# Strassen's scheme for one more unit's q, k, v projection, GpSimd allowed for the weights' low halves, and new priorities and waits in a planned kernel

## The chip, the cores and the metric

The kernel runs on one core of one Trainium2 chip. The metric is device time in microseconds (us), lower is better. The kernel before took 1135.82 us (median of 3 runs, 1135.46 to 1136.92).

## The reference

Two pairs of layers act on x of 2048 rows (tokens) by 640 columns. Each pair is an attention layer and an MLP layer, both with a layer norm in front and a residual sum behind. The attention is local and dilated: a token at position s looks at the 8 positions s, s-2, ..., s-14, in 32 heads of 20 columns. Both pairs use the same weights.

```
for layer in (A, B, A, B):          # A: attention, B: MLP
    A: q, k, v = layernorm(x) @ wqkv            # 640 -> 3 * 640
       logits  = sum(q[s] * k[s - 2 j]) / sqrt(20),  j = 0..7, masked where s - 2 j < 0
       x = x + (softmax(logits) . v[s - 2 j]) @ wo
    B: h = gelu(layernorm(x) @ w1 + b1)         # 640 -> 1536
       x = x + h @ w2 + b2                      # 1536 -> 640
```

All is float32. The kernel keeps the accuracy with pairs of float16: every matmul operand is split into a high half (the value rounded to float16) and a low half (what is left), and a product is three float16 matmuls: high by high, high by low, low by high.

## The kernel before, in words

**Units.** The 2048 rows are cut into 4 units of 512 rows (even or odd positions, first or second half), and the two pairs of layers make 8 units of work, numbered 0 to 7: units 0 to 3 are the first pair of layers, 4 to 7 the second, and unit 4 works on the rows of unit 0 when the MLP of unit 0 is done. A unit has 4 tiles of 128 rows, and its heads are taken in 4 groups of 8 heads (160 columns each of q, k and v). There are thus 32 attention groups.

**The steps of a unit.** The layer norm (`layernorm`) runs mostly on ScalarE (ACT): sums with `accum_out`, then the normalized rows, then their high half; the low half is a subtraction on VectorE (DVE, L648) or on GpSimd (POOL). DMA transposes bring the halves to `yT`. TensorE (PE) multiplies with the weights `wq` (L904, `qkv`), ACT evicts the result to `ev` (L924), a DMA writes it to a DRAM buffer `spill`, and two DMAs fetch it back with the neighbours that the window needs. The attention of a group is a chain on DVE (`attention`): the products of q and k (L998), their sum over each head (L1003), the softmax's small steps (L1010 to L1017, with the exponential on ACT), the products with v (L1019), three sums over the window (L1024 twice, L1027), and the low half of the output (L1035, on DVE or POOL). `project` transposes the output by DMA and multiplies it with `wo` on PE (L1056); its banks are first filled with x by ACT (L1068). Then comes the layer norm for the MLP and the MLP itself (`mlp`): 12 steps per unit of an inner product of 15 matmuls (L1123), a gelu and a rounding on ACT (L1129, L1132), a low half on DVE or POOL (L1134), and an outer product of 24 matmuls (L1144) into five accumulation banks `acc0` to `acc4`, the rest of the columns of all four tiles lying in `acc4`. Units 6 and 7 do their MLP together at the end, by Strassen's scheme (`pair`, `joint`).

**How the banks of the MLP go from unit to unit.** There is one set of the five banks. For units 0, 1 and 2 DVE adds each bank to x (L1188: `acc4` first, then `acc0` to `acc3`), and the next unit's outer product may start on a bank when DVE has read it. For the units from 3 on ACT writes x into the banks ahead (L1104 for `acc0` to `acc3`, L1106 for `acc4`), the outer product adds to that, and ACT takes the sum out. So the first matmul of unit 3's outer product waits for two drains on DVE (`acc4` and `acc0` of unit 2) and the two fills on ACT behind them.

**Strassen for q, k, v.** For the units of the list SEVEN (before: 5, 6 and 7) `qkv7` takes seven products P1 to P7 in place of eight, over two tiles of rows and two groups of columns at a time (L832): 54 matmuls of 480 columns for such a block, four blocks in a unit. A plain unit takes 15 matmuls for each of 16 pairs of tile and group. The scheme needs sums of rows, made on DVE (L679 to L686) and split once more (L706 on ACT, L708 on DVE or POOL), sums of the outputs on DVE (L864, four in a unit), and sums of weights. `factors` makes these after the last plain unit has used the weights: it writes the weights to DRAM (L749), loads pieces of the raw weights (L758), combines them on DVE (L766) and splits them on ACT and DVE (L778, L780).

**The weights of the MLP and of wo** are split once, early on (`prep_rows`, 29 tiles of 128 by 640): ACT writes the high half, 64 times the weight rounded (L500), and DVE writes 64 times the weight minus the high half in one instruction (L501). The MLP's weights then go to DRAM and come back from there.

**What sets the order.** The program is written down as a list of operations with an engine, an estimated duration, a priority, what they need and what buffers they use. `Plan.run` makes a list schedule of it with its own clock: each engine takes the operation that can start first, and between equals the one with the lower priority number. The instructions are then emitted in the order of the planned starts, and on the chip each engine goes through its own list in that order, waiting wherever the next one isn't ready. An operation made with `either` may go to DVE or to POOL; POOL takes it only while DVE is in a sum over heads (L1003), and HOLD says how long DVE leaves it alone first. AHEAD says how far the inner products of the MLP may run ahead of the outer ones.

Of the kernel before, what the change touches and what calls it, by code (L numbers as in the profile page):

```python
# [11 lines left out]
AF = mybir.ActivationFunctionType  # L12
# [11 lines left out]
WS = 64.0  # L24
# [14 lines left out]

AHEAD = 1.5  # L40

# [6 lines left out]

SEVEN = (5, 6, 7)
KH = 2  # L50
# [18 lines left out]

HOLD = {'s': 0.0, 'hlo': 2.0, 'a': 12.0, 'b': 0.0, 'xb': 50.0, 'ol': 12.0, 'ol3': 0.0}  # L70

# [6 lines left out]
class Plan:  # L78
# [49 lines left out]
    def run(self):  # L128
# [172 lines left out]
        order.sort(key=lambda o: o["at"])  # L301
        self.time = max(clock.values())
        self.order = order
        return order
# [15 lines left out]
def sliding_dilated_then_mlp_kernel(  # L320
# [115 lines left out]
    def act(n, prio, emit, need=(), give=(), use=(), table=None, ptr=0, acc=0):  # L436
        plan.add("act", a_cost(n, ptr, acc), prio, emit, need, give, use, table)
# [61 lines left out]
    def split(hi, lo, src):  # L499
        return (lambda: nc.scalar.activation(hi(), src(), AF.Copy, scale=WS),  # L500
                lambda: nc.vector.scalar_tensor_tensor(lo(), src(), WS, hi(), op0=OP.mult, op1=OP.subtract))  # L501
# [18 lines left out]
    def prep_rows(name, key, prio, src, hi, lo, use=(), first=0):  # L520
        def load():
            st = tile_of(*key)
            st = st.rearrange("p a c -> p (a c)").bitcast(FT) if len(st.shape) == 3 else st
            w = src()
            nc.sync.dma_start(st.rearrange("p (k c) -> p k c", k=w.shape[1]) if len(w.shape) == 3 else st, w)

        def raw():
            st = tile_of(*key)
            return st.rearrange("p a c -> p (a c)").bitcast(FT) if len(st.shape) == 3 else st

        dma(P * D * 4 / 1e3, prio, load, need=[("ev", 0, M - 1, 0)], give=[("st", name)], use=[key],
            packet=4 * P if name[0] == "m" and not name[2] else 4 * D)
        a, v = split(hi, lo, raw)
        act(D, prio + first, a, need=[("st", name)], give=[("hi", name)], use=[key, *use])
        dve(D, LOP, v, need=[("hi", name)], give=[("lo", name)], use=[key, *use])

# [33 lines left out]
    def layernorm(n, prio, yk, twice):  # L570
# [11 lines left out]
        def first(t):  # L582
            return prio if n or twice else (-1100, -995, -899, -898)[t]
# [45 lines left out]
        for t in range(m):  # L629
# [13 lines left out]
            if n == 0 and not twice:  # L643
# [3 lines left out]
                need=[("y", name, t)], give=[("yh", name, t)], use=[key, nk, hk])  # L647
            either(D, HOLD['b' if twice else 'a'], first(t), lambda eng, key=key, parts=parts: eng.tensor_sub(parts()[:, 1], tile_of(*key), parts()[:, 0]),  # L648
                need=[("yh", name, t)], give=[("yl", name, t)], use=[key, nk, hk])
# [92 lines left out]
    def factors():  # L742
# [3 lines left out]
        for p in range(2):  # L746
            for q, (g, k) in ORIGIN.items():
                size = 1 if q[0] == "R" else 2
                dma(P * size * 2 * C * 2 / 1e3, -22, lambda p=p, q=q, g=g, k=k, size=size: nc.sync.dma_start(  # L749
                    ws[p, q], flat(wq[:, 2 * p + g, k:k + size])), need=[("wq", 2 * p + g, i) for i in range(3)] + [("out", 0, NF - 1, 0) if p else ("qkvp", SEVEN[0] - 1, M - 1, 1)],  # L750
                    give=[("ws", p, q)], packet=size * 4 * C)
        gone = [("ws", 1, q) for q in ORIGIN]
        for p in (1, 0):
            for j in range(2):
# [12 lines left out]

                dve(4 * C, -24, combine, need=[("fr", p, j, i) for i in range(4)], give=[("fs", p, j)], use=[ak], more=0.2)
                for i, n in enumerate((3, 1)):
                    def part(a, i=i, j=j, p=p):  # L770
                        if p:
                            return wq[:, 2, 3, a] if i else wq[:, 2, :3, a]
                        return wq[:, 2, 2 + j, a] if i else wq[:, 1:4, j, a]

                    def whole(i=i, raw=raw):
                        return raw[3] if i else wq_blocks[:, A0:A0 + 6 * C].bitcast(FT).rearrange("p (i c) -> p i c", c=C)

                    act(n * C, -24, lambda part=part, whole=whole: nc.scalar.activation(part(0), whole(), AF.Copy, scale=WS),  # L778
                        need=[("fs", p, j), *plain(p)], give=[("fh", p, j, i)], use=[ak, tk])
                    dve(n * C, -24, lambda part=part, whole=whole: nc.vector.scalar_tensor_tensor(  # L780
                        part(1), whole(), WS, part(0), op0=OP.mult, op1=OP.subtract),
                        need=[("fh", p, j, i)], give=[("fl", p, j, i)], use=[ak, tk])
# [18 lines left out]
    def qkv7(n):  # L801
# [5 lines left out]
        for s, (p, b) in enumerate(order):  # L807
# [4 lines left out]
            e0, e1 = ("ev", (n, g0, b)), ("ev", (n, g1, b))  # L812
            prio = -500 + n + 0.01 * s

# [68 lines left out]
    def qkv(n):  # L883
# [10 lines left out]
        for k, (g, b) in enumerate(halves):  # L894
            ek = ("ev", (n, g, b))
            for i in range(2):
# [9 lines left out]

                prio, done = (-500 if n != NU - 1 else 13) + n + 0.01 * k, ("qkvp", n, t, g)
                if n or g:
# [642 lines left out]
    for n in range(N):  # L1551
        if n:
            layernorm(n, -100 + n, ("yT", ("a", n)), False)
        qkv(n)
        for g in range(NG):
            fetch(n * NG + g)
            attention(n * NG + g)
        project(n)
        layernorm(n, -150 + n, ("yT", ("b", n)), True)

# [43 lines left out]
```

## Time and profile before

| | |
|---|---|
| runs | 1135.46, 1135.82, 1136.92 us; median 1135.82 |
| the profiled execution | 1137.4 us; its span, from the first to the last instruction, 1135.6 us |
| PE busy | 1121.8 us, 99% of the span |
| DVE busy | 1043.6 us, 92% |
| ACT busy | 648.4 us, 57% |
| POOL busy | 149.9 us, 13% |
| granted PE clock | 1.000 on average |

The span is one execution under the profiler; the 1.8 us between its span and its time lie around the first and the last instruction. Matmuls overlap in the pipeline, so a matmul's own duration is longer than what it adds to a row of them; a chain row with a count gives what a group costs in sequence.

### The profile page before, as it was taken

What the parts mean: (1) busy time and instruction counts of PE and PEld (TensorE: products, weight loads), DVE (VectorE), ACT (ScalarE), POOL (GpSimd) and SP (SyncE); (2) the same over time, 40 slices, a digit from 0 to 9 for tenths busy, and PEclk for the clock granted to TensorE, in tenths of its full rate; (3) what the DMA queues carried; (4) which work ended last, traced back from release to release, by engine and by line L of the source; (5) the groups of instructions that cost most, each with busy time, mean ns of one, the idle gap of its engine ahead of it and who ended that gap; (6) DMA issues with size and microseconds to landing.
All of it is one profiled execution on the core that took longest, in us unless ns stands there. A gap on an engine that the chain in (4) does not pass through costs nothing.

```text
span 1135.6 us, 16918 instructions
## 1 busy us (share of the span) xinstructions
PE 1121.8 (99%) x6560; PEld 603.4 (53%) x6560; DVE 1043.6 (92%) x878; ACT 648.4 (57%) x1187; POOL 149.9 (13%) x109
## 2 busy tenths in 40 slices
PE   8999999999999999999999999999999999999998
PEld 6444455456554565455445544456446555645476
DVE  7999999999999999999999999999989995768972
ACT  6357356647572283757576773478636733857720
POOL 1105001302221011102011311121001210100000
PEclk9999999999999999999999999999999999999999
DMA  9999786678877859769787798567797756695101
GB/s 308 301 331 247 218 213 162 209 261 231 257 263 204 224 176 316 251 200 256 200 297 217 192 258 291 192 197 183 193 334 210 218 172 162 156 268 161 43 25 70
DMA packets 257564, 246.05 MB, mean 217 GB/s; under 512 B 150524, under 2 KB 215116, under 8 KB 257484
## 3 DMA queue, kind: packets, MB, share of 16 engines
q1 hardware_dynamic: 257484, 244.98, 73.6%
q8 instruction: 51, 0.84, 0.3%
q14 instruction: 29, 0.24, 0.1%
HBM read 157.55 MB, written 52.64 MB: 185 GB/s over the span
## 4 chain that ended last, share of the span: by engine, by line
PE 67%; DVE 21%; issue 5%; DMA 4%; ACT 2%; SPq 0%; POOLq 0%; POOL 0%; DVEq 0%; ACTq 0%
PE ps L904 20%; PE ps L1123 14%; PE acc L1144 12%; PE ps L1056 8%; PE ps L832 6%; DVE sm L1003 4%; DVE pr L1019 4%; PE acc L1325 3%; DVE pr L998 3%; PE ps L1360 2%; PE ps L1325 2%; DVE pr L1024 2%; DVE pr L1257 1%; DVE w L708 1%; DMA yT<-w 1%
## 5 line engine op out<-in xcount | busy, mean ns | idle before, releaser
L1144 PE MATMUL acc<-c,act 128*128 128x512 f16 (+1 forms) x1728 | 248.9, 299 | 0.2
L904 PE MATMUL ps<-wq,yT 128*128 128x480 f16 (+1 forms) x1230 | 245.6, 361 | 1.5 <-ACT wq L500 1.1
L1123 PE MATMUL ps<-yT,c 128*128 128x512 f16 x1080 | 243.7, 379 | 0.0
L1144 PEld LDWEIGHTS <-act 128*128 128x128 f16 x1728 | 135.9, 98 | 110.0 <-issue 0.4
L904 PEld LDWEIGHTS <-yT 128*128 128x128 f16 x1230 | 118.7, 98 | 124.9 <-issue 1.3
L1019 DVE TENSOR_TENSOR pr<-sm,v 128x5120 f32<-128x5120 f32 x32 | 175.5, 5485 | 0.4
L998 DVE TENSOR_TENSOR pr<-qk 128x5120 f32<-128x5120 f32 x32 | 175.5, 5483 | 0.4
L1003 DVE TENSOR_REDUCE sm<-pr 128x256 f32<-128x5120 f32 x32 | 175.2, 5476 | 0.1
L1123 PEld LDWEIGHTS <-c 128*128 128x128 f16 x1080 | 103.7, 98 | 121.5 <-DVE c L501 0.3
L1024 DVE TENSOR_TENSOR pr<-pr 128x2560 f32<-128x2560 f32 x64 | 137.6, 2150 | 0.2
L1056 PE MATMUL ps<-wo,yT 128*128 128x320 f16 x960 | 131.9, 299 | 1.9 <-ACT ps L1068 1.9
L1056 PEld LDWEIGHTS <-yT 128*128 128x128 f16 x960 | 93.8, 98 | 39.6 <-issue 1.6
L924 ACT ACTIVATE ev<-ps 128x480 f32<-128x480 f32 x80 | 45.4, 569 | 109.1 <-PE ps L904 108.6
L1129 ACT ACTIVATE act<-ps,b 128x512 f32<-128x512 f32 x72 | 49.3, 685 | 99.9 <-PE ps L1123 98.7
L615 POOL TENSOR_TENSOR ln<-ln,half 128x2 f32<-128x2 f32 (+1 forms) x31 | 57.9, 1869 | 346.1 <-ACT ln L612 346.1
L832 PE MATMUL ps<-wq,yT 128*128 128x480 f16 x396 | 85.1, 366 | 2.0 <-ACT ps L850 1.8
L841 ACT ACTIVATE ev<-ps 128x480 f32<-128x480 f32 x72 | 39.9, 567 | 52.2 <-PE ps L832 50.1
L832 PEld LDWEIGHTS <-yT 128*128 128x128 f16 x396 | 38.2, 98 | 43.0 <-issue 2.7
L832 PE MATMUL ps<-wq 128*128 128x480 f16 x252 | 54.5, 366 | 0.8 <-ACT ev L841 0.8
L1035 POOL TENSOR_TENSOR ohl<-w,ohl 128x640 f16<-128x640 f32 x17 | 23.8, 1403 | 204.5 <-DVE sm L1015 45.3
L602 ACT ACTIVATE junk<-xf,ln 128x640 f16<-128x640 f32 x57 | 46.8, 820 | 0.5
L1132 ACT ACTIVATE act<-act 128x512 f16<-128x512 f32 x72 | 45.1, 626 | 1.4
(221 smaller groups left out, 1269.4 us busy)
## 6 DMA issues: line engine op xcount, KB each, us to landing
c<-mw SPq DMA_DIRECT2D x126, 320.0 KB, 3.6
spill<-ev SPq DMA_DIRECT2D x64, 480.0 KB, 3.9
qk<-spill SPq DMA_DIRECT2D x32, 880.0 KB, 6.1
v<-spill SPq DMA_DIRECT2D x32, 880.0 KB, 5.2
qk<-spill SPq DMA_DIRECT2D x32, 320.0 KB, 3.5
c<-in_B_w_dram SPq DMA_DIRECT2D x24, 320.0 KB, 5.1
mw<-c SPq DMA_DIRECT2D x24, 320.0 KB, 4.8
pr<-in_B_w_dram SPq DMA_DIRECT2D x24, 320.0 KB, 3.9
```

The source lines that it names most:

```text
L615: pool(0.5, prio, lambda t0=t0, t1=t1: nc.gpsimd.tensor_tensor(col(2)[:, t0:t1], col(2)[:, t0:t1], half[:, t0:t1], op=OP.pow), need=[("vr" ...
L832: nc.tensor.matmul(ps, r(x_, j), w[:, j, y_], start=start and i == 0, stop=i == len(todo) - 1, skip_group_check=True)
L904: nc.tensor.matmul(ps, transposed(yk)[:, a * KD + k, t * P:(t + 1) * P], wq[:, g, k, b, i0 * GC:i1 * GC], start=first and j == 0, stop=las ...
L998: nc.vector.tensor_mul(pr.rearrange("p w t c -> p w (t c)"), w[:, HALO + m:HALO + 2 * m].rearrange("p t c -> p (t c)")[:, None, :].to_broa ...
L1003: dve(E, G - 0.7, lambda: nc.vector.tensor_reduce(by_key(), heads(), axis=AX.X, op=OP.add), need=[("qk", G)], give=[("lg", G)], use=[*pk, sk])
L1019: dve(E, G - 0.85, lambda: nc.vector.tensor_mul(heads(), by_key()[:, :, :, None].to_broadcast([P, W, m * GH, DH]), windows(tile_of(*vw), [ ...
L1024: dve(m * w * GC, G - 0.9, lambda w=w: nc.vector.tensor_add(pr[:, 0:w], pr[:, 0:w], pr[:, w:2 * w]), need=[last], give=[("ad", G, w)], use=vk)
L1056: nc.tensor.matmul(tile_of(*pk)[:, :D // 2], transposed(yk)[:, a * KD + k, t * P:(t + 1) * P], wo[:, b, k, c * D // 2:(c + 1) * D // 2], s ...
L1123: nc.tensor.matmul(tile_of(*pk)[:, :nt], tile_of(*ck)[:, a, k * P:(k + 1) * P], transposed(yk)[:, c * KD + k, t0 * P:t1 * P], start=i == 0 ...
L1129: act(nt, -430, lambda pk=pk, h32=h32, e=e: nc.scalar.activation(tile_of(*h32)[:, :nt], tile_of(*pk)[:, :nt], AF.Gelu_apprx_tanh, bias=b1[ ...
L1144: nc.tensor.matmul(accs[k][:, c0:c0 + n], tile_of(*hk)[:, a, (i - t0) * P:(i - t0 + 1) * P], tile_of(*wk)[:, c, w0:w0 + n], start=first, s ...
L1325: nc.tensor.matmul(tile_of(*to(i))[:, :HALF], hl()[:, a, i * P:(i + 1) * P], row(c), start=start and (a, c) == PASS[0], stop=(a, c) == PAS ...
```

## The change

It does five things.

- Unit 4 joins SEVEN, so its q, k, v go through `qkv7`, its rows through `sums_of_rows`, and the sums of weights in `factors` are due between unit 3's and unit 4's projections, where they were due between unit 4's and unit 5's.
- In `prep_rows` ACT first scales the raw weights in place (a new instruction), then rounds them; the low half becomes a plain subtraction made with `either`, so that POOL may take it. In the new file these are lines 542, 543 and 544.
- The priorities of the projections and of the layer norms are tables by unit (QKV_AT, ROWS_AT, INNER_AT) in place of formulas; PREP_AT takes the place of a number with the same value.
- HOLD gets new values, with one by unit for the low halves of the layer norm (HOLD_A); AHEAD goes from 1.5 to 2.5.
- The store of the second half of the plain weights waits for the first outer product of the MLP's first step, where it waited for the last step of unit 0.

```diff
-AHEAD = 1.5
+AHEAD = 2.5
-SEVEN = (5, 6, 7)
+SEVEN = (4, 5, 6, 7)
-HOLD = {'s': 0.0, 'hlo': 2.0, 'a': 12.0, 'b': 0.0, 'xb': 50.0, 'ol': 12.0, 'ol3': 0.0}
+HOLD = {'lo': 0, 's': 2, 'hlo': 0, 'b': 0, 'xb': 50, 'ol': 12, 'ol3': 5}
+
+PREP = 0
+
+QKV_AT = (-500, -499, 2, 9, -20, 6, 2, -493)
...
+HOLD_A = (0, 12, 0, 20, 12, 12, 6, 20)
+PREP_AT = -24
...
-        a, v = split(hi, lo, raw)
-        act(D, prio + first, a, need=[("st", name)], give=[("hi", name)], use=[key, *use])
-        dve(D, LOP, v, need=[("hi", name)], give=[("lo", name)], use=[key, *use])
+        act(D, prio + first, lambda: nc.scalar.activation(raw(), raw(), AF.Copy, scale=WS), need=[("st", name)], give=[("sc", name)], use=[key, *use])
+        act(D, prio + first, lambda: nc.scalar.activation(hi(), raw(), AF.Copy), need=[("sc", name)], give=[("hi", name)], use=[key, *use])
+        either(D, HOLD["lo"], LOP, lambda eng: eng.tensor_sub(lo(), raw(), hi()), need=[("hi", name)], give=[("lo", name)], use=[key, *use])
...
-            either(D, HOLD['b' if twice else 'a'], first(t), ...
+            either(D, HOLD['b'] if twice else HOLD_A[n], first(t), ...
...
-need=[...] + [("out", 0, NF - 1, 0) if p else ("qkvp", SEVEN[0] - 1, M - 1, 1)],
+need=[...] + [("outh", 0, PREP, 0) if p else ("qkvp", SEVEN[0] - 1, M - 1, 1)],
...
-            prio = -500 + n + 0.01 * s
+            prio = QKV_AT[n] + 0.01 * s
...
-                prio, done = (-500 if n != NU - 1 else 13) + n + 0.01 * k, ("qkvp", n, t, g)
+                prio, done = QKV_AT[n] + 0.01 * k, ("qkvp", n, t, g)
...
-            layernorm(n, -100 + n, ("yT", ("a", n)), False)
+            layernorm(n, ROWS_AT[n], ("yT", ("a", n)), False)
...
-        layernorm(n, -150 + n, ("yT", ("b", n)), True)
+        layernorm(n, INNER_AT[n], ("yT", ("b", n)), True)
```

The new plan moves nearly every instruction. Two places are shown. In the new file the lines behind `prep_rows` are numbered 9 higher: L1188 became L1197, L1003 L1012, L1144 L1153, L1123 L1132.

On DVE, the drain of unit 2's MLP banks into x. Before (`sm` is the softmax's buffer, `pr` the attention's products, `ev` the sums of Strassen's outputs, `v` the fetched values):

```order
L1015 TENSOR_REDUCE sm1_88<-sm1_88 128x32
L1016 RECIPROCAL sm0_87<-sm0_87 128x32
L1188 SCALAR_TENSOR_TENSOR xf_65<-acc4_100,xf_65 128x4x128
L1188 SCALAR_TENSOR_TENSOR xf_65<-acc0_96,xf_65 128x512
L864 TENSOR_TENSOR ev2_71<-ev2_71,ev1_70 128x960
L1017 TENSOR_TENSOR sm0_87<-sm0_87 128x256
L1016 RECIPROCAL sm1_88<-sm1_88 128x32
L1019 TENSOR_TENSOR pr_95<-sm0_87,v0_68 128x5120
L1017 TENSOR_TENSOR sm1_88<-sm1_88 128x256
L1188 SCALAR_TENSOR_TENSOR xf_65<-acc1_97,xf_65 128x512
L1188 SCALAR_TENSOR_TENSOR xf_65<-acc2_98,xf_65 128x512
```

The same place on DVE in the changed kernel:

```order
L1036 TENSOR_TENSOR w4_86<-pr_95 128x640
L1143 TENSOR_TENSOR act_66<-act_66 128x512
L1025 RECIPROCAL sm1_88<-sm1_88 128x32
L1007 TENSOR_TENSOR pr_95<-qk0_67 128x5120
L1026 TENSOR_TENSOR sm1_88<-sm1_88 128x256
L1143 TENSOR_TENSOR act_66<-act_66 128x512
L1012 TENSOR_REDUCE sm0_87<-pr_95 128x8x32
L1197 SCALAR_TENSOR_TENSOR xf_65<-acc4_100,xf_65 128x4x128
L1143 TENSOR_TENSOR act_66<-act_66 128x512
L1197 SCALAR_TENSOR_TENSOR xf_65<-acc0_96,xf_65 128x512
L1197 SCALAR_TENSOR_TENSOR xf_65<-acc1_97,xf_65 128x512
```

The drain stood among the softmax steps of attention groups 18 and 19; now it stands right behind the sum over heads of group 20 (counted from 0), the 21st L1003 of the program.

On PE, the start of unit 3's outer product, the first matmul of which is the one into `acc0` below. Before:

```order
L1056 LDWEIGHTS yT2_74
L1056 MATMUL ps2_94<-wo_102,yT2_74 128x320
L1144 LDWEIGHTS act_66
L1144 MATMUL acc0_96<-c22_81,act_66 128x512
L1144 LDWEIGHTS act_66
L1144 MATMUL acc4_100<-c22_81,act_66 128x128
```

The same place on PE in the changed kernel:

```order
L1132 LDWEIGHTS c10_76
L1132 MATMUL ps1_93<-yT2_74,c10_76 128x512
L1153 LDWEIGHTS act_66
L1153 MATMUL acc0_96<-c21_80,act_66 128x512
L1153 LDWEIGHTS act_66
L1153 MATMUL acc4_100<-c21_80,act_66 128x128
```

Before, five inner products of unit 3 and unit 4's output projection (L1056) stood ahead of it; now it stands behind four inner products of unit 3 and ahead of unit 4's output projection. The Strassen blocks of unit 5 are ahead of it in both.

## Rows read from the trace of the kernel before

**Rows 1.** Page, part 1: busy us, share of the span, instructions; part 2, DVE.
```profile
PE 1121.8 (99%) x6560; PEld 603.4 (53%) x6560; DVE 1043.6 (92%) x878; ACT 648.4 (57%) x1187; POOL 149.9 (13%) x109
...
DVE  7999999999999999999999999999989995768972
```

**Rows 2.** Who PE waited for: us in total, times, longest us.
```profile
PE ps L1056 <- ACT ps L1068: 1.9, 2, 1.1
PE ps L832 <- ACT ps L850: 1.8, 1, 1.8
PE acc L1325 <- ACT act L1332: 1.4, 1, 1.4
...
PE ps L832 <- ACT ev L841: 0.8, 1, 0.8
```

**Rows 3.** The chain that ended last: start us, us, what, in order of time.
```profile
157.54 16.30 PE ps L1056 x120
173.84 24.30 PE ps L904 x120
198.14 9.71 PE ps L1123 x45
207.85 3.26 PE acc L1144 x24
...
346.95 48.60 PE ps L904 x240
```

**Rows 4.** Timeline of PE at unit 7's output projection: start us, us.
```profile
964.28 16.46 PE L1056 MATMUL ps<-wo,yT 128*128 128x320 f16 x120
```

**Rows 5.** DVE by stretch: length, busy us (instructions), granted clock, DMA share, GB/s.
```profile
0.00:36.00 36.00, 26.57 (x57) 1.00 0.98 314
0.00:614.59 614.59, 599.37 (x448) 1.00 0.82 242
614.59:953.66 339.07, 322.35 (x220) 1.00 0.74 218
```

**Rows 6.** Timeline of DVE at attention group 20's sum over heads.
```profile
614.59 5.48 DVE L1003 TENSOR_REDUCE sm<-pr 128x256 f32<-128x5120 f32 x1
619.98 0.42 DVE L683 TENSOR_TENSOR w<-w,w 128x256 f32<-128x256 f32 x1
```

**Rows 7.** DVE by line and shape: busy us, mean ns of one, idle before it.
```profile
L1019 DVE TENSOR_TENSOR pr<-sm,v 128x5120 f32<-128x5120 f32 x32 | 175.5, 5485 | 0.4
...
L1024 DVE TENSOR_TENSOR pr<-pr 128x2560 f32<-128x2560 f32 x32 | 90.1, 2817 | 0.1
L1024 DVE TENSOR_TENSOR pr<-pr 128x1280 f32<-128x1280 f32 x32 | 47.4, 1482 | 0.2
...
L501 DVE SCALAR_TENSOR_TENSOR c<-c,c 128x640 f16<-128x640 f32 x24 | 19.0, 818 | 1.3 <-ACT c L500 1.3
L864 DVE TENSOR_TENSOR ev<-ev,ev 128x960 f32<-128x960 f32 x12 | 13.8, 1152 | 4.9 <-ACT ev L841 4.9
...
L1188 DVE SCALAR_TENSOR_TENSOR xf<-acc,xf 128x512 f32<-128x512 f32 x15 | 9.7, 682 | 0.7 <-PE acc L1144 0.6
...
L684 DVE TENSOR_TENSOR w<-w 128x256 f32<-128x256 f32 x6 | 2.5, 425 | 0.2
```

**Rows 8.** ACT by line and shape, in the same columns.
```profile
L500 ACT ACTIVATE c<-c 128x640 f16<-128x640 f32 x24 | 17.2, 730 | 19.1 <-DMA c<-in_B_w_dram 12.1 <-DVE c L501 4.2 <-PE ps L1123 2.5
...
L1104 ACT ACTIVATE acc<-xf 128x512 f32<-128x512 f32 x12 | 6.7, 597 | 1.0 <-DVE xf L1188 1.0
```

**Rows 9.** Who DVE waited for: us in total, times, longest us.
```profile
DVE sm L1015 <- ACT sm L1013: 5.8, 6, 2.8
```

**Rows 10.** Timeline between the last attention group and unit 7's output projection.
```profile
952.83 0.83 DVE L1035 TENSOR_TENSOR ohl<-w,ohl 128x640 f16<-128x640 f32 x1 [2.16 <-ACT ohl L1032]
...
959.24 0.78 ACT L1068 ACTIVATE ps<-xf 128x320 f32<-128x320 f32 x2
```

**Rows 11.** All engines by stretch: PE, PEld, DVE, ACT, POOL busy, PE clock, DMA, GB/s.
```profile
560.00:575.00 15.00, 13.19 (x77) 6.65 (x75) 14.93 (x11) 7.53 (x12) 4.26 (x3) 1.00 0.93 242
```

More of the change, by code (lines that the diff above doesn't have):

```diff
@@ L68 @@
 PAIRS = ("qk", "pv", "ad", "o", "sub", "at", "hlo", "yl", "xb", "ol", "wq", "lo", "lm")
-HOLD = {'s': 0.0, 'hlo': 2.0, 'a': 12.0, 'b': 0.0, 'xb': 50.0, 'ol': 12.0, 'ol3': 0.0}
+HOLD = {'lo': 0, 's': 2, 'hlo': 0, 'b': 0, 'xb': 50, 'ol': 12, 'ol3': 5}
+PREP = 0
+QKV_AT = (-500, -499, 2, 9, -20, 6, 2, -493)
+ROWS_AT = (-500, -199, -98, -17, -96, -95, -194, -93)
+INNER_AT = (-150, -49, -698, -47, -696, -45, -694, -43)
+HOLD_A = (0, 12, 0, 20, 12, 12, 6, 20)
+PREP_AT = -24
 TURN = 2.7
@@ L302, in run @@
         self.time = max(clock.values())
+        self.when = when
         self.order = order
@@ L647, in layernorm @@
                 need=[("y", name, t)], give=[("yh", name, t)], use=[key, nk, hk])
-            either(D, HOLD['b' if twice else 'a'], first(t), lambda eng, key=key, parts=parts: eng.tensor_sub(parts()[:, 1], tile_of(*key), parts()[:, 0]),
+            either(D, HOLD['b'] if twice else HOLD_A[n], first(t), lambda eng, key=key, parts=parts: eng.tensor_sub(parts()[:, 1], tile_of(*key), parts()[:, 0]),
                 need=[("yh", name, t)], give=[("yl", name, t)], use=[key, nk, hk])
@@ L749, in factors @@
                 dma(P * size * 2 * C * 2 / 1e3, -22, lambda p=p, q=q, g=g, k=k, size=size: nc.sync.dma_start(
-                    ws[p, q], flat(wq[:, 2 * p + g, k:k + size])), need=[("wq", 2 * p + g, i) for i in range(3)] + [("out", 0, NF - 1, 0) if p else ("qkvp", SEVEN[0] - 1, M - 1, 1)],
+                    ws[p, q], flat(wq[:, 2 * p + g, k:k + size])), need=[("wq", 2 * p + g, i) for i in range(3)] + [("outh", 0, PREP, 0) if p else ("qkvp", SEVEN[0] - 1, M - 1, 1)],
                     give=[("ws", p, q)], packet=size * 4 * C)
@@ L766, in combine @@
                         nc.vector.tensor_sub(to, a, b)
-                dve(4 * C, -24, combine, need=[("fr", p, j, i) for i in range(4)], give=[("fs", p, j)], use=[ak], more=0.2)
+                dve(4 * C, PREP_AT, combine, need=[("fr", p, j, i) for i in range(4)], give=[("fs", p, j)], use=[ak], more=0.2)
                 for i, n in enumerate((3, 1)):
@@ L776, in whole @@
                         return raw[3] if i else wq_blocks[:, A0:A0 + 6 * C].bitcast(FT).rearrange("p (i c) -> p i c", c=C)
-                    act(n * C, -24, lambda part=part, whole=whole: nc.scalar.activation(part(0), whole(), AF.Copy, scale=WS),
+                    act(n * C, PREP_AT, lambda part=part, whole=whole: nc.scalar.activation(part(0), whole(), AF.Copy, scale=WS),
                         need=[("fs", p, j), *plain(p)], give=[("fh", p, j, i)], use=[ak, tk])
-                    dve(n * C, -24, lambda part=part, whole=whole: nc.vector.scalar_tensor_tensor(
+                    dve(n * C, PREP_AT, lambda part=part, whole=whole: nc.vector.scalar_tensor_tensor(
                         part(1), whole(), WS, part(0), op0=OP.mult, op1=OP.subtract),
```

## The prediction

> **What bounds the kernel now.** The page's first part comes first: PE is busy 99% of the span and DVE 92%, and DVE's tenths stand at 9 from the second slice to the twenty-ninth [rows 1]. Two engines are full at once there, so neither can be judged alone. PE's waits are next: behind the start it waits 1.9, 1.8 and 0.8 us for ACT in the units' work and 1.4 us in the joint MLP at the end [rows 2]; the units' waits come to about 4.5 us. So PE is paid by its matmuls, and a matmul taken out shortens the span if nothing that PE needs comes later than before. What decides is DVE: in its first 36 us it is idle 36.0 - 26.6 = 9.4 us, in the first 614.59 us 15.2 us in all, and from there to the end of the last attention group, at 953.66, 16.7 us [rows 5]. Its idle time up to 614.59 is the start and gaps of a tenth of a microsecond; there is no reserve in it. The reserve lies behind.
>
> **The change part by part.**
>
> *Unit 4 by Strassen, on PE.* 16 x 15 = 240 matmuls of 480 columns become 4 x 54 = 216. 240 of them took 48.60 us [rows 3], so one is 0.2025 us and 24 are 4.9 us. All of it is on PE's own path.
>
> *The same, on DVE and ACT.* Unit 4 adds on DVE two times five row sums (four of 256 columns and one of 128), 2 more low halves of 640 and 2 of 256 (some go to POOL), and 4 sums of outputs. An instruction takes its row's mean less about 0.08 us, by which it overlaps the next (5.48 shown, 5.39 from start to start [rows 6]). Counted in the two DVE orders up to the last attention group's low half, the new one has 3 subtractions of 640 more (2.2 us), two sets of sums (3.1), 4 sums of outputs at 1.07 (4.3), 6 low halves of the MLP at 0.60 (3.6), and 4 low halves of weights (3.0), one of the attention's output and one b2 addition (1.5) less: 8.8 us more [rows 7]. DVE, already full, is given nearly twice what PE is relieved of.
>
> *The weights' split.* 29 more ACT instructions at 0.73 us are 21 us [rows 8]. ACT is busy 57%, and DVE waited for the split of the MLP's weights only 1.3 us in 24 tiles [rows 7], since loads run ahead. I put it at 0; if every tile's wait doubled it would cost 1.3 us. It cannot gain, as the path from load to low half only gets longer. A plain subtraction costs what the scaled one did, and of the 29 only 4 go to POOL, the others staying on DVE.
>
> *The order.* Here it is decided, at the first matmul of unit 3's outer product (the second pair of order pieces). PE up to there: the order is the old one up to 198.14, when the first inner product starts [rows 3]. Then the new queue has 8 plain q, k, v tiles (24.3 us, 120 matmuls), 40 inner products at 9.71 / 3 = 3.24 (129.5), 36 outer products at 3.26 (117.4), two Strassen units (2 x 216 x 0.2025 = 87.5) and three output projections at 16.30 (48.9) [rows 3]: 407.6 us. Without any wait PE is there at 605.7.
>
> DVE up to there: the matmul needs DVE's second drain of unit 2. Counted up to and with it, the new DVE order has, against the old one up to the start of the 21st L1003 at 614.59 [rows 6]: more, that L1003 itself (5.39), 4 sums of outputs (4.29), six low halves of 640 (4.43) and one of 256 (0.34), five row-sum groups' instructions (2.8) and a low half of the MLP (0.60), 17.9 in all; less, one product with v (5.40), the two sums behind it (2.74, 1.40), the last sum and its low half (1.48), 4 low halves of weights (2.95), three drains (1.8) and a b2 addition (0.74), 16.5 in all [rows 7]. That is 1.4 us more work, so with the same idle time the drain ends at 616.0. A fill on ACT follows (0.60 [rows 8]), and two handovers between engines that I put at 0.1 together: PE starts at 616.7, eleven microseconds behind the 605.7 that its own work allows, where the old PE had lost 3.7 by the same count. The wait will not lie at this one matmul: the drains of units 0 and 1 and the sums of unit 4's outputs come late in the same way and take their parts of it ahead.
>
> The rest: behind it the new PE queue has 32 inner (103.6) and 36 outer products (117.4), two Strassen units (87.5) and four output projections (65.2), 373.7 us. Before, unit 7's output projection started at 964.28 [rows 4]; with it (16.3) and three outer products (9.8) the units' work was done at 990.4, and the joint MLP and the end took the remaining 1135.6 - 990.4 = 145.2. That part is not changed. 616.7 + 373.7 + 145.2 = 1135.6: the old span to a tenth. The 4.9 us and the old waits are given back in full as waits for DVE.
>
> Two small terms: Strassen blocks wait for ACT between their steps now and then (0.8 in unit 6 or 7 before [rows 2]), say +0.8; and a wait of DVE for the exponential, 5.8 us in six before [rows 9], may go in part, as the new order puts more between its two sides, say -0.6. Sum +0.2 on a span of 1135.6 and on an execution of 1137.4; the runs' median is 1.6 below that execution, so I forecast 1135.82 + 0.2 = **1136.0 us**.
>
> *AHEAD and HOLD* act through the order alone; their price is in the counts. That the low halves of the MLP now come one inner product (3.24 us) earlier ahead of their use costs nothing on PE.
>
> **The rivals.**
>
> *A: faster, DVE is less late than counted.* Each microsecond that DVE reaches the drain earlier comes off the end, until the 605.7 is reached. At 3 us, the time is 1133. Without any wait before the joint MLP it would be 605.7 + 373.7 + 145.2 = 1124.6, 11 below; with the old 4.5 us, 1129.1, so 1129.3 as a median. For it: all named waits of DVE up to 614.59 could go, and POOL has room. Against it: 9.4 of the 15.2 us is the start, which isn't touched, and the remainder is spread in small gaps [rows 5].
>
> *B: slower, DVE misses the last projection.* Unit 7's projection stands 346.4 us of PE work behind the drain point (373.7 less 16.3, less 3 outer products and 3/8 of one), at 963.1. It needs the last low half 6 us earlier (its end at 953.66, the first fill at 959.24 and a matmul behind [rows 10]), at 957.1. DVE's 8.8 us more put that end at 962.5 if its idle time behind 614.59 stays at 16.7 us: PE then waits 5.4 us more and the time is 1141.4. It decides as soon as more than 11.3 of the 16.7 us remain. For it: PE, now late, makes DVE wait for gelus and for Strassen's outputs of unit 7, as it did before for 4.9 us [rows 7]. Against it: the new order starts these earlier on PE.
>
> *C: slower, by PE's clock.* Before, the longest wait in the units' work was 1.8 us and the clock stayed at 1.00, the 2.4 GHz level, through it [rows 2, 11]. Waits of 3 to 4 us in one piece may let it fall to 1.2 GHz; a group of 15 matmuls would then take twice 3.24, so 3.2 us for each such wait, and with two of them 1142. The Trainium skill, page "TensorE: Matmul & The Clock Gate", section "HAM oscillation — how this bites in real kernels", says that waits between bursts of matmuls bring the throttled clock back and that each burst then starts cold; no wait in this trace is long enough to show it, and by that rule this rival would hold wherever the wait at a drain comes in one piece.
>
> **How the numbers follow.** What a measurement of this kernel can tell from no change is about 0.2%, 2.3 us: 1133.5 to 1138.1. The likeliest case, waits in place of matmuls, 0.42, has that range as its own. A has 0.27. B has 0.19, C 0.08, and DVE's start made longer by the weights' split 0.04: slower 0.31. For 8 in 10 I take 1130.5, most of A but not a kernel free of waits, to 1141.5, B in full.
>
> **What would show it.** Right: PE has some 4.9 us less matmul time, and waits grow by about as much or more: L1153 for L1197 (the drains), L841 for ACT behind L873, L1056 for its fills, most of them between 320 and 620 us, and none of this size behind. Unit 3's first outer product starts near 616 to 617, unit 7's output projection near 963. DVE's idle time up to the drain is near 15 us, and DVE's busy time rises by 8 to 10 us. B shows as a wait of L1056 of several microseconds near 960; C as a granted clock below 1.00 in a stretch between 320 and 620. The forecast is wrong if unit 3's first outer product starts before 614 or after 619, for then DVE's count or its idle time is wrong; and if DVE is late but the end isn't, for then the joint MLP gave time back, which I count as fixed.

## The result: slower by 4.2 us, and the profile after

The changed kernel takes 1140.57 us (median of 6 runs, 1139.51 to 1141.82), the kernel before in the same series 1136.37 us (1135.46 to 1138.76): a ratio of 1.0035, 95% interval 1.0022 to 1.0047. The forecast was 1136.0 us and no change; the time lies inside the range given, on its slow side.

The profiled execution of the changed kernel is the fastest of its six (1139.51 us, span 1137.7), that of before one of its slower (1137.4, span 1135.6), so the spans differ by 2.1 us only. The page's first part answers to [rows 1]: 24 matmuls fewer, and yet PE is as busy as before; DVE has 7.2 us more, where 8 to 10 were forecast.

```profile
PE 1121.7 (99%) x6536; PEld 603.1 (53%) x6536; DVE 1050.8 (92%) x894; ACT 665.4 (58%) x1226; POOL 163.8 (14%) x111
```

Who PE waited for (us in total, times, longest us) answers to [rows 2]. Each of the first two rows holds a wait longer than any of before, where none was over 1.8 us; the second row has no counterpart there.

```profile
PE ps L1065 <- ACT ps L1077: 5.6, 3, 4.4
PE ps L1132 <- issue: 2.6, 1, 2.6
...
PE ps L841 <- ACT ev L850: 1.1, 2, 0.7
...
PE acc L1153 <- ACT acc L1113: 0.3, 1, 0.3
```

The windows behind these two waits (start and end, length, busy us of PE, PEld, DVE, ACT and POOL, granted clock, DMA share, GB/s), and DVE's work up to the point on which the forecast stood:

```profile
0.00:613.43 613.43, 606.16 (x3453) 318.75 (x3454) 601.56 (x458) 359.81 (x672) 98.68 (x76) 1.00 0.85 252
...
318.00:320.00 2.00, 2.00 (x6) 0.72 (x5) 2.00 (x3) 0.00 (x0) 0.75 (x1) 0.50 1.04 419
...
646.00:648.00 2.00, 0.07 (x1) 0.10 (x1) 1.97 (x6) 0.40 (x1) 0.50 (x1) 1.00 1.12 209
648.00:650.40 2.40, 0.00 (x0) 0.00 (x0) 2.40 (x5) 2.37 (x5) 0.00 (x0) 0.66 1.09 206
...
652.00:654.00 2.00, 2.00 (x9) 1.19 (x8) 2.00 (x1) 1.29 (x2) 0.00 (x0) 0.50 1.40 52
656.00:658.00 2.00, 2.00 (x17) 1.43 (x16) 2.00 (x1) 0.74 (x2) 0.00 (x0) 1.00 0.87 260
```

PE stood still from 646 to 650.4, and the clock granted to it fell in that time to 0.50, the 1.2 GHz level, and stayed there until after 654: 9 matmuls in 2 us where 17 went later. Unit 4's output projection so takes 18.8 us from its start to that of the next matmul, against 16.3 [rows 3]. In the same way the three inner products behind the wait at 316.5 take 11.39 us, against 9.71 for three [rows 3]. The spans' difference is thus told by three terms: 24 matmuls, -4.9; the waits in the list of who PE waited for, 12.7 against 9.9 us in all, +2.8; the low clock, 2.5 + 1.7 = +4.2. The sum is +2.1. It says where PE's time lies, and not what would be gained if a term were taken away; smaller gaps are left out of it (with them PE's idle time rises by 2.2 us, from 13.8 to 16.0).

Now the longer wait, followed back. The timeline around it (start us, us, engine, line, operation, in brackets the idle time before it and what ended it):

```profile
620.17 2.83 DVE L1033 TENSOR_TENSOR pr<-pr 128x2560 f32<-128x2560 f32 x1
620.87 11.76 POOL L624 TENSOR_TENSOR ln<-ln,half 128x2 f32<-128x2 f32 x1 [10.84 <-ACT ln L621]
622.90 0.70 DVE L1143 TENSOR_TENSOR act<-act 128x512 f16<-128x512 f32 x1
...
623.50 1.50 DVE L1033 TENSOR_TENSOR pr<-pr 128x1280 f32<-128x1280 f32 x1
624.90 0.70 DVE L1143 TENSOR_TENSOR act<-act 128x512 f16<-128x512 f32 x1
625.50 0.83 DVE L1036 TENSOR_TENSOR w<-pr 128x640 f32<-128x640 f32 x1
...
626.24 0.43 DVE L1020 TENSOR_TENSOR sm<-sm 128x256 f32<-128x256 f32 x1
...
626.58 5.50 DVE L1007 TENSOR_TENSOR pr<-qk 128x5120 f32<-128x5120 f32 x1
...
632.66 0.48 ACT L629 ACTIVATE ln<-ln 128x1 f32<-128x1 f32 x2 [8.73 <-POOL ln L624]
...
633.31 0.69 POOL L624 TENSOR_TENSOR ln<-ln,half 128x2 f32<-128x2 f32 x1 [0.68 <-ACT ln L621]
...
639.76 0.69 DVE L1143 TENSOR_TENSOR act<-act 128x512 f16<-128x512 f32 x1 [7.69 <-ACT act L1141]
...
647.60 0.74 ACT L715 ACTIVATE w<-w 128x640 f16<-128x640 f32 x1 [4.22 <-DVE w L694]
...
649.97 0.78 ACT L1077 ACTIVATE ps<-xf 128x320 f32<-128x320 f32 x2
650.45 18.97 PE L1065 MATMUL ps<-wo,yT 128*128 128x320 f16 x120 [4.37 <-ACT ps L1077]
```

Read it from above. L624 is the power -0.5 that turns variances into 1/sigma, on two columns, for the first layer norm of unit 6. On two columns it takes 0.69 us at its shortest, as at 633.31, and here 11.76. DVE runs seven TENSOR_TENSORs without a gap from 620.17 to 632.08 (626.58 + 5.50), and the power ends 0.55 us behind the last. ACT's next instruction needs the power and waits 8.73 us; everything behind it on ACT waits too, the gelus and high halves of unit 3's MLP among them; so DVE runs dry and waits 7.69 us for one of them, and its row sums for unit 6 are late in turn (L694, for which ACT waits 4.22); the fill of unit 4's output projection stands behind those on ACT, and PE waits 4.37 us. DVE went idle at 632.08, and the power ended 0.55 us later: the stall freed itself. The row of this line over the whole run (count, then shortest, median and longest ns; the shortest is one of the five on a single column) has the power once at twice the longest of before, which was 5692 ns:

```profile
L624 POOL TENSOR_TENSOR ln<-ln,half x31: 556/1568/11762, 13.7 to 989.7; 128x2 f32<-128x2 f32 x26, 128x1 f32<-128x1 f32 x5
```

Last, the point named as decisive, unit 3's first outer product: it starts at 613.43, on the fill that follows DVE's drain, with next to no wait.

```profile
612.05 2.49 DVE L1197 SCALAR_TENSOR_TENSOR xf<-acc,xf 128x512 f32<-128x512 f32 x4
612.77 0.60 ACT L1113 ACTIVATE acc<-xf 128x512 f32<-128x512 f32 x1 [0.54 <-DVE xf L1197]
613.43 0.97 PE L1153 MATMUL acc<-c,act 128*128 128x512 f16 x6 [0.28 <-ACT acc L1113]
```

### The profile page after: what moved, and what is told of

Read it like the earlier page. It is cut to its first block, busy times and chain, and to the rows that moved or that the text cites. A ratio compares the mean times of both kernels' runs of the same rounds, so it can differ in the third digit from the quotient of the medians.

```text
span 1137.7 us, 17017 instructions
## 1 busy us (share of the span) xinstructions
PE 1121.7 (99%) x6536; PEld 603.1 (53%) x6536; DVE 1050.8 (92%) x894; ACT 665.4 (58%) x1226; POOL 163.8 (14%) x111
## 5 line engine op out<-in xcount | busy, mean ns | idle before, releaser
L1153 PE MATMUL acc<-c,act 128*128 128x512 f16 (+1 forms) x1728 | 250.9, 299 | 0.5 <-ACT acc L1113 0.3
L1132 PE MATMUL ps<-yT,c 128*128 128x512 f16 x1080 | 246.3, 381 | 3.1 <-issue 2.6
L913 PE MATMUL ps<-wq,yT 128*128 128x480 f16 (+1 forms) x990 | 196.6, 360 | 0.4 <-ACT wq L509 0.4
L1153 PEld LDWEIGHTS <-act 128*128 128x128 f16 x1728 | 136.7, 98 | 112.1 <-issue 0.9
L1012 DVE TENSOR_REDUCE sm<-pr 128x256 f32<-128x5120 f32 x32 | 175.3, 5478 | 0.2
L1132 PEld LDWEIGHTS <-c 128*128 128x128 f16 x1080 | 103.4, 98 | 126.0 <-issue 5.1
L913 PEld LDWEIGHTS <-yT 128*128 128x128 f16 x990 | 95.4, 98 | 98.5 <-issue 0.5
L1065 PE MATMUL ps<-wo,yT 128*128 128x320 f16 x960 | 134.7, 302 | 5.6 <-ACT ps L1077 5.6
L624 POOL TENSOR_TENSOR ln<-ln,half 128x2 f32<-128x2 f32 (+1 forms) x31 | 69.1, 2229 | 356.0 <-ACT ln L621 355.9
L1065 PEld LDWEIGHTS <-yT 128*128 128x128 f16 x960 | 94.7, 99 | 45.1 <-issue 5.8
L841 PE MATMUL ps<-wq,yT 128*128 128x480 f16 x528 | 112.2, 366 | 1.1 <-ACT ev L850 1.1
L850 ACT ACTIVATE ev<-ps 128x480 f32<-128x480 f32 x96 | 53.6, 567 | 75.4 <-PE ps L841 72.8
L841 PEld LDWEIGHTS <-yT 128*128 128x128 f16 x528 | 51.1, 98 | 54.9 <-issue 1.5
L841 PE MATMUL ps<-wq 128*128 128x480 f16 x336 | 72.0, 366 | 0.0
L933 ACT ACTIVATE ev<-ps 128x480 f32<-128x480 f32 x64 | 36.1, 566 | 58.6 <-PE ps L913 58.1
L1143 DVE TENSOR_TENSOR act<-act 128x512 f16<-128x512 f32 x64 | 43.6, 685 | 10.6 <-ACT act L1141 10.6
```

Source lines behind the costliest of these rows:

```text
L624: pool(0.5, prio, lambda t0=t0, t1=t1: nc.gpsimd.tensor_tensor(col(2)[:, t0:t1], col(2)[:, t0:t1], half[:, t0:t1], op=OP.pow), need=[("vr" ...
L841: nc.tensor.matmul(ps, r(x_, j), w[:, j, y_], start=start and i == 0, stop=i == len(todo) - 1, skip_group_check=True)
L850: act(C, -400 + n, lambda: nc.scalar.activation(to(), tile_of(*bank)[:, :C].rearrange("p (a c) -> p a c", a=3), AF.Copy, scale=1.0 / WS), ...
L913: nc.tensor.matmul(ps, transposed(yk)[:, a * KD + k, t * P:(t + 1) * P], wq[:, g, k, b, i0 * GC:i1 * GC], start=first and j == 0, stop=las ...
L1012: dve(E, G - 0.7, lambda: nc.vector.tensor_reduce(by_key(), heads(), axis=AX.X, op=OP.add), need=[("qk", G)], give=[("lg", G)], use=[*pk, sk])
L1065: nc.tensor.matmul(tile_of(*pk)[:, :D // 2], transposed(yk)[:, a * KD + k, t * P:(t + 1) * P], wo[:, b, k, c * D // 2:(c + 1) * D // 2], s ...
```

## The experiments

Theory 1: the extra time is the power that DVE holds up, with the low clock behind its wait. Theory 2, the prediction's own: DVE is too full, and a wait taken away in one place comes back in another. Times are medians. They come from three series, in which the kernel before had 1136.8 us (beside the copy, the 40 matmuls more, the hold put back and the list alone), 1136.21 us (the reciprocal, the 24 copies, the split undone and the numbers alone) and 1136.14 us (the three kernels with less work).

**Let the power through.** One instruction more on DVE, behind the L1143 of 622.90:

```diff
-lambda: nc.gpsimd.tensor_tensor(col(2)[:, t0:t1], ..., op=OP.pow)
+lambda: (nc.gpsimd.tensor_tensor(col(2)[:, t0:t1], ..., op=OP.pow),
+         n == 6 and not twice and t0 == 0 and nc.vector.tensor_copy(bn[:, 0, :2], col(2)[:, :2]))
```

> The changed kernel with one DVE copy of two elements more, which reads the result of GpSimd's power for unit 6's first layernorm and stands on DVE behind the low half of the MLP at 622.9 us, so that DVE has to let the power through there; all else keeps its order. Theory 1 (the power is locked out by DVE): the power of 11.8 us takes under 3.5 us, ACT no longer waits 8.7 us behind it, DVE not 7.7 us at 639.8, unit 4's output projection starts without its wait of 4.4 us and so at the full clock (16.4 instead of 18.8 us): 4.4 + 2.5 = 6.9 us off, 1133.7 us. Theory 2 (DVE has too much work, and any wait only changes its place): the wait at the projection goes but comes back within the next 300 us, 1139 to 1141 us. Theory 3 (the power was late for another reason, such as its instruction's arrival): DVE now waits at the copy for 8 us and more, and the time is 1140 us or longer.

Measured: 1133.02 us (1132.58 to 1133.54), 7.55 less than the changed kernel and 0.9964 of before (0.9952 to 0.9977). In its timeline DVE waits 0.59 us at the copy, the power takes 3.29 us, ACT waits 0.25, and the projection starts without a wait and runs at full clock:

```profile
621.32 3.29 POOL L624 TENSOR_TENSOR ln<-ln,half 128x2 f32<-128x2 f32 x1 [10.83 <-ACT ln L621]
624.64 0.48 ACT L629 ACTIVATE ln<-ln 128x1 f32<-128x1 f32 x2 [0.25 <-POOL ln L624]
624.64 0.17 DVE L625 COPY bn<-ln 128x2 f32<-128x2 f32 x1 [0.59 <-POOL ln L624]
646.36 16.46 PE L1065 MATMUL ps<-wo,yT 128*128 128x320 f16 x120
```

Theory 1 expected 6.9 us off, and nothing of it comes back later. So the whole loss, and more, was this one instruction: without its stall the change is a gain.

**Does DVE have to wait, or is a gap enough?** The same place, another instruction:

```diff
-nc.vector.tensor_copy(bn[:, 0, :2], col(2)[:, :2])
+nc.vector.reciprocal(bn[:, 0, :2], half[:, :2])
```

> As the kernel with the one copy more, but in the copy's place on DVE stands a reciprocal of two constants, which waits for nothing and has one input, so DVE doesn't wait for the power. Theory gap (any instruction of DVE with one input lets the power through): the power takes about 3 us as with the copy, 1133 us. Theory wait (only idle time of DVE lets it through in this stretch): the power takes 11 to 12 us as in the changed kernel, and the time is 1140 to 1141 us.

Measured: 1132.28 us (1131.93 to 1132.36), ratio 0.9962 (0.9949 to 0.9974), the fastest kernel that leaves nothing out. The timeline holds the test twice:

```profile
621.38 3.29 POOL L624 TENSOR_TENSOR ln<-ln,half 128x2 f32<-128x2 f32 x1 [10.84 <-ACT ln L621]
623.42 0.69 DVE L1143 TENSOR_TENSOR act<-act 128x512 f16<-128x512 f32 x1
624.02 0.16 DVE L625 RECIPROCAL bn<-half 128x2 f32<-128x2 f32 x1
625.36 8.78 POOL L624 TENSOR_TENSOR ln<-ln,half 128x2 f32<-128x2 f32 x1 [0.68 <-ACT ln L621]
627.16 5.49 DVE L1007 TENSOR_TENSOR pr<-qk 128x5120 f32<-128x5120 f32 x1
633.17 0.42 DVE L688 TENSOR_TENSOR w<-w 128x256 f32<-128x256 f32 x1
633.50 0.41 DVE L1024 TENSOR_REDUCE sm<-sm 128x32 f32<-128x256 f32 x1
```

The first power ends at 624.67, 0.56 us behind the L1143 and while DVE goes on: 0.16 us of an instruction with one input let it through. That it must be one with one input is not shown by itself: no run puts an equally short one with two inputs there. The next power then meets a run of seven TENSOR_TENSORs, takes 8.78 us, and ends 0.55 us behind the last of them (633.59), when DVE has come to a reduction. ACT waits 1.77 us for that one and PE not at all. The Trainium skill, page "SBUF — State Buffer", states that a VectorE instruction with two SBUF inputs contends with a GpSimd instruction that reads SBUF (section "Who interferes with whom"), and that whichever starts first gets the shared ports for the whole instruction while the other blocks (section "SBUF: two separate sides"). The trace agrees, and shows more: in a run of such instructions it can stay blocked behind one after the other.

**Is it the clock?** 40 short matmuls ahead of unit 4's projection, into unused columns of its first bank (which changes what the projection adds to there):

```diff
-i = 0
+i = fill(nc, tile_of(*pk)[:, D // 2:], wo[:, 0, 0]) if (n, t, c) == (4, 0, 0) else 0
```

> The changed kernel with 40 matmuls of 192 columns (about 3.3 us at the full clock) put on PE ahead of unit 4's output projection, into the unused 192 columns of its first output bank: they need nothing that the projection waits for, so they fill most of its wait of 4.4 us, and the wait itself stays. Theory clock: the projection behind them runs at 2.4 GHz from its start and takes 16.4 instead of 18.8 us: 2.5 us off, 1138.1 us. Rival: the 2.5 us come from the projection's own fills on ACT or from contention, and it takes 18.8 us as before: 1140.6 us, or up to 3 us more where the wait is shorter in this run.

Measured: 1143.3 us. The fillers didn't run in the wait: they waited for the same fill. So the test is another than was meant, and it still tells the theories apart:

```profile
651.30 5.86 PE L1617 MATMUL ps<-wo 128*128 128x192 f16 x40 [4.37 <-ACT ps L1077]
657.00 16.46 PE L1065 MATMUL ps<-wo,yT 128*128 128x320 f16 x120
```

Whatever comes first behind the wait pays for it (5.7 us from start to start, at a granted clock of 0.50 from 651.3 to 655, for matmuls that would take some 3.3 us at the full clock, an estimate by columns from [rows 3]), and the projection behind it runs at full speed. The loss follows PE's wait, not the projection's fills. The power took 11.76 us in this run again.

**The prediction's own step: does DVE set unit 3's start?** Three kernels, all on the one with the reciprocal. In the first, 40 matmuls are taken out of PE's queue; in the second, 4.7 us out of DVE's; the third has both.

```diff
-for a, b in PASS:
+for a, b in PASS[:2 + (n != 3)]:          # the projection of unit 3
...
```
```diff
+V = 1 if G == 17 else W                   # windows of the product of q and k
-nc.vector.tensor_mul(pr..., ... [P, W, m * GC] ...)
+nc.vector.tensor_mul(pr...[:, :V], ... [P, V, m * GC] ...)
```

> The kernel with the reciprocal (1132.28 us), in which unit 3's output projection, at 534 us, leaves out 40 of its 120 matmuls (one of the three passes; its output then lacks the weights' low halves): 5.4 us less work on PE at a place where PE waits for nothing. The order is kept. Theory DVE (unit 3's first outer product starts when DVE's drain of unit 2 lets it, as the prediction had it): it still starts at 613.9 us within 0.5, PE waits 5 to 6 us in front of it and may lose 1 to 2.5 us more by a low clock behind that wait: 1132.3 to 1135 us. Theory PE: it starts 5.4 us earlier, and the time is 1126.9 us.

> The kernel with the reciprocal, in which DVE computes only one of the eight windows of one product of queries and keys (group 17, between 500 and 560 us; 640 instead of 5120 columns): 4.7 us less work on DVE. The order is kept. Theory both (PE reaches unit 3's first outer product 0.3 us ahead of DVE's drain, so DVE alone has nothing to give): the time stays within 0.7 us of 1132.3. Theory DVE alone: 4.7 us off, 1127.6 us.

> Both edits together: 40 matmuls less on PE in unit 3's output projection and 4.7 us less on DVE in group 17. Theory both: unit 3's first outer product starts 4.5 to 5 us earlier, near 609.2, and the time is 1127.5 us, more than either edit gives alone. Theory PE: 1126.9 us, no other than with the matmuls alone. Theory DVE: as with DVE's edit alone.

Measured: 1132.04, 1131.38 and 1130.27 us, against 1132.28. PE's timeline of the first: 4.1 of the 5.4 us come back as waits between 547 and 559, and at the outer product the wait for the drain has grown by 0.5.

```profile
548.05 1.38 PE L841 MATMUL ps<-wq,yT 128*128 128x480 f16 x6 [1.90 <-ACT xf L1082]
550.19 3.81 PE L841 MATMUL ps<-wq,yT 128*128 128x480 f16 x18 [0.76 <-ACT xf L1082]
...
614.98 0.97 PE L1153 MATMUL acc<-c,act 128*128 128x512 f16 x6 [0.83 <-ACT acc L1113]
```

The same matmul in the second, where PE no longer waits for it, and in the third:

```profile
613.34 0.98 PE L1153 MATMUL acc<-c,act 128*128 128x512 f16 x6
```
```profile
611.76 0.97 PE L1153 MATMUL acc<-c,act 128*128 128x512 f16 x6 [0.82 <-ACT acc L1113]
```

So matmuls taken from PE alone buy nothing (-0.2 us), DVE's work alone 0.9, both together 2.0. That is more than the two apart, as two engines that bound the same stretch should give, but far from the 4.7 that "both" expected: DVE gave part of its gain back in a wait of 2.9 us for ACT at 520, and PE kept 2.2 us of its waits between 547 and 556. ACT's order looks like a third bound there. In all four profiled executions the time less the start of this matmul is within 0.1 us of 518.4 (1132.32 - 613.94 with the reciprocal alone, then 1133.44 - 614.98, 1131.73 - 613.34 and 1130.14 - 611.76), so this start is what the time follows. The execution of the first kernel that was profiled is its slowest: it is 1.04 us late at this matmul, and was so at 446 us already, before the matmuls that were taken out.

**All the powers let through.** 24 copies instead of the one (`n > 1` in place of the condition).

> The changed kernel with such a copy behind 24 of its powers on GpSimd, not the one alone; the order is otherwise kept. Theory 1 (only the one power that held ACT up costs time): DVE loses up to 24 times some 0.7 us in idle time and copies, of which it can bear some up to 613 us, so the time is that of the single copy or longer, 1133 to 1140 us. Rival (the other powers of 3 to 6 us hold the kernel up too): below 1132 us.

Measured: 1136.44 us, ratio to before 1.0001 (0.9992 to 1.0009): 3.4 us slower than with one copy. Unit 3's first outer product starts at

```profile
617.15 0.97 PE L1153 MATMUL acc<-c,act 128*128 128x512 f16 x6 [0.62 <-ACT acc L1113]
```

which is 3.3 us later than with one (613.88). Up to it DVE is busy 2.2 us more and idle 1.0 us more. What DVE loses ahead of this point goes to the end whole, as the prediction had it; and no gain from the other long powers shows.

**The weights' split undone**, on the kernel with the copy, all else in the same order (in short, not the code itself):

```diff
-act(raw * WS -> raw); act(raw -> hi); lo = raw - hi
+act(raw * WS -> hi); lo = raw * WS - hi        # for the 25 low halves on DVE
```

> The kernel with the one copy more (1133.02 us), and besides the late weights are split in one ACT step as before the change: 25 of the 29 scaling steps on ACT are left out (the four whose low half is on GpSimd keep theirs), and the low half takes the scale itself. The order of all else is kept. Theory ACT (the scaling steps stand in ACT's full queue between 285 and 309 us, ahead of the rows of unit 1's inner layernorm): the last rows are turned 1.5 to 2 us earlier, PE's wait of 2.0 us at 316.4 falls under 0.7 us, and the time to 1130 to 1131.5 us. Rival (the prediction's: the steps cost nothing, as loads run ahead): the wait stays at 2 us and the time at 1133 us within 0.5 us.

Measured: 1132.88 us against 1133.02. PE's wait ahead of unit 1's inner products is 1.93 us instead of 2.04:

```profile
315.66 2.53 PE L1132 MATMUL ps<-yT,c 128*128 128x512 f16 x11 [1.93 <-issue]
```

25 ACT steps of 0.73 us less, and the time is the same: the split costs nothing, as forecast. ACT's last row came 1.2 us earlier (L655 at 306.88, not 308.06), but its low half stood in DVE's queue and came 0.6 us earlier only (L657 at 309.38, not 310.01).

**Parts of the change, planned anew.** Three kernels with one list or number put back; the planner then makes another order.

```diff
-HOLD = {..., 'ol3': 5}                    # on the changed kernel
+HOLD = {..., 'ol3': 0}
```
```diff
-SEVEN = (5, 6, 7)                         # on the kernel before
+SEVEN = (4, 5, 6, 7)
```
```diff
-SEVEN = (4, 5, 6, 7)                      # on the changed kernel
+SEVEN = (5, 6, 7)
```

> The changed kernel with one number put back: the low half of a unit's last attention group is again taken by DVE at once (a hold of 0 instead of 5 us). The order of all engines is planned anew. Theory 1: unit 1's output projection starts some 6 us earlier than 272.4, the rows of its inner layernorm are turned earlier, and PE's wait of 2.6 us at 316.5 with the low clock behind it (1.5 us) is gone: 4 us off, 1136.5 us, if the power on GpSimd still holds unit 4's projection up; up to 7 us more off if the new order happens to spare it. Theory 2 (DVE too full): the wait is moved, 1139 to 1141 us.

> The kernel before with one edit, unit 4 in the list of units that project by Strassen's scheme; weights' split, holds and priorities stay as they were. Theory 1 (the loss lies in the new numbers of the plan): the 4.9 us of matmuls come off unless a wait of the same kind as those of the changed kernel happens to arise, 1131.5 us. Theory 2 (DVE has no room for unit 4's added work): all of it is given back, 1136 to 1137 us, as the prediction had it, with PE's waits grown by 4 to 5 us.

> The changed kernel with unit 4 taken out of the list of Strassen units again: the new split of the weights, holds, priorities and AHEAD stay. Theory 1 (the loss is one power on GpSimd and a few late rows, set by chance of the order): the order is planned anew, so those two waits need not arise; the 4.9 us of matmuls come back; 1134 to 1142 us, around 1138. Theory 2 (DVE has no room for unit 4's sums): without them DVE is 7 us freer and the time falls below that of the kernel before, to 1131 to 1134 us.

Measured: 1144.28, 1185.13 and 1160.69 us; both theories missed in all three, by far in the last two. Their longest waits of PE, in this order:

```profile
323.83 8.51 PE L1132 MATMUL ps<-yT,c 128*128 128x512 f16 x26 [6.07 <-DMA yT<-w]
```
```profile
PE ps L1056 <- DMA yT<-ohl: 29.0, 1, 29.0
```
```profile
PE ps L841 <- ACT ps L859: 17.9, 2, 15.9
```

With the hold put back unit 1's projection starts at 282.2, not earlier than 272.4, and the wait grows: this number alone didn't make the wait at 316.5. In this kernel no power takes longer than 5.69 us, so the stall is gone, and yet it is slower than the changed one: another order brings other waits. With unit 4 by Strassen in the old numbers, DVE makes sums and splits of the weights between 320 and 425 us (16 of L766 and 8 of L780, 19.6 us), and unit 2's projection waits 29 us for attention; how much of it is theirs was not taken apart. With the new numbers but unit 4 plain, one Strassen block waits 15.9 us. So the list and the numbers belong together: neither 1136.4, the list alone 1185, the numbers alone 1161, both 1140.6. What one of them is worth by itself can't be told from these.

## Why the prediction was wrong, and where right

**The step that failed** is "the rest": behind unit 3's first outer product PE was given 373.7 us of work and no wait ("none of this size behind"). The wait of 4.4 us at unit 4's projection, with 2.5 us of low clock, lies there. Its cause is an engine that the prediction counted only as room ("POOL has room"): a GpSimd instruction of two columns, which the change neither added nor touched, but which the new order put under a run of seven DVE instructions. Shown by the copy and the reciprocal: 7.5 and 8.3 us off with one instruction more.

**Luck.** That the time lies inside the range is luck. It lies outside the 1133.5 to 1138.1 of the likeliest case, the upper end of 1141.5 was set for rival B, which didn't occur, and two misses of opposite sign stand in it: 3.3 us less for DVE's lateness and some 7.5 to 8.3 more for the stall, 1140.2 to 1141.0 from the forecast's 1136.0.

**The term that was mis-sized** is DVE's lateness. The forecast took over the idle time of before, 15.2 us [rows 5], and came to 616.7 for that outer product; in the changed kernel DVE is idle 613.43 - 601.56 = 11.9 us up to it. These 3.3 us are the whole difference to the measured 613.43, and the forecast's own mark, "wrong if unit 3's first outer product starts before 614", said so. I had refused this in rival A with the words that the idle time was the start and small gaps. But 0.8 us came off the start, and the rest was not only "gaps of a tenth of a microsecond": in the trace of before DVE waits 0.8 us at 166, 0.6 at 312 and 0.9 at 560, and these waits did go.

**What held.** The main step, that DVE's drain comes last at unit 3's start: 40 matmuls taken out buy nothing, and DVE's lost time is passed on whole. But it comes last by 0.3 us only, with PE and ACT close behind: with 4.7 us less work DVE's drain of `acc0` to `acc3` began 0.95 us earlier (611.62, not 612.57), PE no longer waited for it, and the time fell by 0.9. The waits that bring PE so close were foreseen ahead of that point; they lie at 316 and 416 to 445, none of them at a drain, and they are free: in the kernel with the copy PE waits 2.0 us at 316.4 at full clock, in that with the reciprocal 2.7 us and then runs 1.7 us slower, and unit 3 starts at 613.88 and 613.94. The sum of the rest: 518.9 us forecast; 1131.1 - 613.88 = 517.2 measured with the copy. The matmuls: 24 fewer. The weights' split: nothing. So the prediction's sum with DVE 3.3 us less late is rival A at "1133", and that is what the two kernels without the stall take.

**The rivals.** A was the true state of DVE, hidden under the stall. B did not occur: unit 7's projection starts at 967.84 without a wait. C, the clock, was right in kind: priced at 3.2 us a wait, measured at 1.7 and 2.5; but it was tied to waits at drains between 320 and 620, and the one that cost lay behind. The Trainium skill, page "TensorE: Matmul & The Clock Gate", section "HAM oscillation — how this bites in real kernels", describes a kernel whose matmuls wait for DMA between bursts, and says that each burst then starts cold. The trace agrees at 650.45 (granted clock 0.50 behind the wait of 4.4 us); behind a wait of 3.04 us at 317.39, in the kernel with less work on DVE, the clock stayed at 1.00.

**Open.** In the changed kernel powers got through at the start of a two-input low half in other places (at 299.22 and 678.43), and not at 622.90; what decides this is not settled, nor, then, how long a run of DVE instructions has to be to hold a power up. Which number of the plan moves unit 1's projection from 259.4 to 272.4 us is not either, but the wait at 316.5 behind it costs nothing at the end. The runs' medians lie 4.2 us apart and the profiled spans 2.1: what its slower executions add is in no trace.

## What to carry to other kernels

Follow every wait of the bounding engine back through the queues, past the first engine named: here PE waited for ACT, ACT for DVE, DVE for ACT, and ACT for 0.7 us of GpSimd work that DVE itself held up. For a tiny operation on GpSimd whose result another engine's queue needs at once, try an instruction with one input near it on DVE; here one of 0.16 us was worth 8.3 us. And when two engines bound the same stretch, work taken from one of them, however rightly counted, buys little until the other is relieved as well.

## What was not expected of the hardware

- A GpSimd instruction of two columns, 0.69 us at its shortest, took 11.76 us under seven DVE instructions with two inputs in a row and 8.78 us under another seven, ended 0.55 us behind the last, and was let through by a DVE instruction of 0.16 us with one input.
- Behind PE's wait near 316 us the granted clock fell to 0.50 in some runs and not in others, with the same order: after waits of 2.56, 2.56, 2.72, 2.81 and 2.90 us the three inner products took 11.4 us, after 1.93, 2.04, 2.62 and 3.04 us they took 9.71. A wait of 2.6 to 3.0 us can cost 1.7 us more, or nothing.
